# Cross attention with an expert layer: turning the first batch's token weights by VectorE and transfers instead of TensorE, and moving the third batch's token steps one group later

## The chip, the cores and the metric

The kernel runs on one core of a Trainium2 chip. The metric is the device time of one execution in microseconds (us). A program on one core has no second die to be compared with, so runs are told apart here by their time and by the mean granted TensorE clock that each run lists. Every repeated run counted as fast; the single runs of the three looks near the end have no state, and there the clock record itself decides.

Names in the profile: PE is TensorE's matmul stream, PEld its weight loads, DVE is VectorE, ACT is ScalarE, SP is SyncE; SPq and ACTq are the issuing of transfers by those two. L283 is line 283 of the kernel. The changed kernel's line numbers are mostly four higher than before: L415, L543, L593, L710, L716 before are L419, L547, L597, L714, L720 after. L197 (scores), L277 (read) and L283 (scaling of the read) are the same in both. The variants of the experiments have numbers of their own: L591 and L620 there are the L597 of the changed kernel, L541 is L547, L601 and L630 are L607, L278 is L277.

## The reference, cut to what matters

```python
# attention: B, H, S, Ns, D = 8, 8, 512, 32, 64, float32
scores  = scale * x @ state.T            # tokens look at states
a       = exp(scores - max); a /= sum + 1e-9
xread   = a @ state
scores2 = scale * state @ x.T            # states look at tokens
a2      = exp(scores2 - max); a2 /= sum + 1e-9
sread   = a2 @ x                         # "the read": needs a2 with tokens on partitions
# then, on concat(xread, sread) as 4608 rows of 512:
h = x @ w_in                             # 512 -> 2048
g = h * erf(softplus(h))
out = g @ w_out                          # 2048 -> 512
```

## The kernel before: the parts that matter here

Token weights `a2` come out of the softmax with states on partitions. The read needs them turned. The first batch turns them on TensorE, eight 128x128 transposes into two PSUM tiles (L261, 0.87 us on the chain); the other batches turn 32x32 blocks on VectorE (L370, 1.23 us) and let 16 transfers put the blocks in place (11.17 us of issuing for the second batch's).

```python
ps_at = ctx.enter_context(tc.tile_pool(name="ps_at", bufs=2, space=PSUM))   # two tiles "at"
...
    def turn_weights(a2):                        # first batch only
        a2T = att.tile([P, 2, NC, P], F32, name="sc")
        for e in range(2):
            ps = ps_at.tile([P, NC, P], F32, name="at")
            for c in range(NC):
                nc.tensor.transpose(out=ps[:, c, :], in_=a2[:, e, P * c:P * c + P],
                                    identity=ident)
            nc.scalar.copy(a2T[:, e], ps)
        return a2T
...
    def read_tokens(b, a2T, z2, pool=ps_at, name="at"):
        ...                                      # 64 small matmuls into one tile "at" (L277)
        for e in range(2):                       # L283 empties it
            nc.vector.tensor_scalar(sn[:, e], sr[:, e], z2[:, e:e + 1], None, op0=ALU.mult)
...
    def mixed_part(b, g, j, parts, ...):         # "mixing": takes both tiles "at"
        ps = [ps_at.tile([P, gw], F32, name="at")[:, 0:n] for _ in range(2)]
        ...
    def soft(i, gT):                             # ACT
        nc.scalar.activation(out=gT[0][:, i], in_=h_t[i], func=ACTF.Softplus)
    def keep_h(i, gT):                           # DVE, L710
        nc.vector.tensor_copy(gT[1][:, i], h_t[i])
    def evict(i, gT, late=False):
        for f in (keep_h, soft) if late else (soft, keep_h):
            f(i, gT)
```

Up to the point where the second batch's groups begin, the order of the source is the order on each engine. After it a scheduler orders the instructions, and steps of the next batch's attention are hung into the groups of matrix work as side steps (`side[k]`). From there on each group of matrix work forms the first layer from seven small products (L487) whose sums VectorE adds; "product two" and "product seven" below are two of them. The output matmuls (L593) of one group run between the products of the next.

Of the kernel before, what the change touches and what calls it, by code (L numbers as in the profile page):

```python
# [8 lines left out]
F32 = mybir.dt.float32  # L9
# [7 lines left out]
def kernel(  # L17
# [17 lines left out]
    nc = tc.nc  # L35
    B, H, S, D = x.shape
    Ns = state.shape[2]
# [187 lines left out]
    def sums(a):  # L225
        z1 = small.tile([P, 2, NC * NI], F32, name="z1")
        for e in range(2):
            nc.vector.reduce_sum(out=z1[:, e], in_=a[:, e], axis=AX.X)
        return z1
# [7 lines left out]
    def largest(sc):  # L237
        m2 = small.tile([P, 2], F32, name="m2")
        for e in range(2):
            nc.vector.reduce_max(out=m2[:, e:e + 1], in_=sc[:, e], axis=AX.X)  # L240
        nc.vector.tensor_scalar(m2, m2, -scale, None, op0=ALU.mult)
        return m2

    def weigh_tokens(sc, m2, a2):

        z2 = small.tile([P, 2], F32, name="z2")
        for e in range(2):
            nc.scalar.activation(out=a2[:, e], in_=sc[:, e], func=ACTF.Exp, bias=m2[:, e:e + 1],
                                 scale=scale, accum_out=z2[:, e:e + 1])
        return z2  # L250

    def inverse(z):
        nc.vector.tensor_scalar(z, z, 1e-9, None, op0=ALU.add)
        nc.vector.reciprocal(z, z)

    def turn_weights(a2):
        a2T = att.tile([P, 2, NC, P], F32, name="sc")
        for e in range(2):
            ps = ps_at.tile([P, NC, P], F32, name="at")
            for c in range(NC):  # L260
                nc.tensor.transpose(out=ps[:, c, :], in_=a2[:, e, P * c:P * c + P],  # L261
                                    identity=ident)
            nc.scalar.copy(a2T[:, e], ps)
        return a2T

    sn_t = {}
# [25 lines left out]
    def attention0(between):  # L292



        xt = x_t[0]
        xT = att.tile([P, NI, S], F32, name="xT")
        xp = [ps_o.tile([P, S], F32, name="o%d" % i) for i in range(3)]
        xp.append(ps_h.tile([P, S], F32, name="h"))
        for c in 1, 0, 2, 3:  # L300
            if c == 2:
                warm(3)
            for i in range(NI):
                nc.tensor.transpose(out=xp[i][:, P * c:P * c + P],
                                    in_=xt[:, c, 2 * i:2 * i + 2, :], identity=ident)
        for i in range(NI):
            (nc.scalar.copy, nc.vector.tensor_copy)[i % 2](xT[:, i, :], xp[i])
        states(range(1))
        s2 = scored(0, xT)
        between[0]()  # L310
        both = att.tile([P, NI, S], F32, name="xT")
        sc = att.tile([P, 2, S], F32, name="sc")
        a = states_weights(0, s2, both)
        for e in range(2):
            nc.scalar.copy(sc[:, e], s2[e])
        between[1]()
        z1 = sums(a)
        between[2]()
        normalise(a, z1)
        for e in range(2):  # L320
            nc.vector.transpose(out=aT[0][:, e], in_=both[:, e])

        def rest():
            a2 = both[:, 2:4]
            m2 = largest(sc)
            yield
            z2 = weigh_tokens(sc, m2, a2)
            inverse(z2)
            yield
            a2T = turn_weights(a2)  # L330
            yield
            read_tokens(0, a2T, z2)
            yield

        return rest()
# [9 lines left out]
    def attention(b, xT=None):  # L345



        turned = []
        if xT is None:  # L350
            xT, *turned = turn_x(b)
        sc, _ = scores(b, xT)
        marks.extend(turned)
        yield
        both = att.tile([P, NI, S], F32, name="xT")
        a = states_weights(b, [sc[:, e] for e in range(2)], both)
        yield
        m2 = largest(sc)
        yield
        z2 = weigh_tokens(sc, m2, both[:, 2:4])  # L360
        yield
        z1 = sums(a)
        inverse(z2)
        yield
        normalise(a, z1)
        for e in range(2):
            nc.vector.transpose(out=aT[b][:, e], in_=both[:, e])
        yield

        nc.vector.transpose(out=both[:, 0:2], in_=both[:, 2:4])  # L370
        a2T = att.tile([P, 2, NC, P], F32, name="sc")
        blocks = both[:, 0:2].rearrange("p e (c m n) -> p m (e c) n", m=NI, n=Ns)
        rows = a2T.rearrange("p e c (i n) -> p i (e c) n", n=Ns)
        for m in range(NI):
            for i in range(NI):
                nc.sync.dma_start(out=rows[Ns * m:Ns * m + Ns, i],
                                  in_=blocks[Ns * i:Ns * i + Ns, m])
        yield
        read_tokens(b, a2T, z2, *((ps_h, "h") if 1 < b < B - 1 else ()))
        if b + 1 < B:  # L380
            load_x(b + 1)
        yield
# [305 lines left out]
    def on_dve(kind, j, ks=range(3)):  # L688
        for k in ks:
            made[kind, j][1][k]()  # L690
            if k == 2:
                fetch()
# [51 lines left out]
    def some0(g, gT, rs, ts):  # L744
        done(project(gT[0], g, acc, rs, ts))
# [94 lines left out]
    def finish_(gT):  # L840
        for i in range(GF):
            erf(slice(i, i + 1), gT)
            times(slice(i, i + 1), gT)

    next(rest)
    finish_(g2)
    next(rest)
    on_dve("o", 5, [2])
    some0(2, g2, range(3), range(2))
    on_act("i", 6)  # L850
    next(rest)
# [2 lines left out]
    on_act("i", 7)  # L854
    m_t[0, 3] = mix.tile([P, 2, gw], F32, name="m")
    mixed_part(0, 3, 0, 2, nc.scalar.copy, nc.scalar.copy)
    xT, _ = turn_x(1)
    some0(2, g2, range(1), range(2, 4))
    on_dve("i", 7, [0, 1])
    next(rest)  # L860
    on_dve("i", 7, [2])
    load_x(1)
    on_act("o", 6)
    on_dve("o", 6, [0, 1])
    turn = attention(1, xT)
# [11 lines left out]
    next(turn)  # L877
    on_dve("o", 6, [2])
    next(turn)
    some0(2, g2, range(1, 2), range(2, 4))  # L880
    for i in 2, 3:
        first0(3, i, g3[0])
        evict(i, g3)
    some0(2, g2, range(2, 3), range(2, 4))
    finish_(g3)
    mixed(1, 2 * begins(1), nc.scalar.copy, nc.scalar.copy)
    some0(2, g2, range(3, 4), range(2, 4))
# [31 lines left out]
    for b in range(1, B + 1):  # L919
        if b < B:  # L920
            groups = fast(b, 2, lambda h, b=b: put_x(b, h))
        else:
            groups = fast(b, 1, lambda h: put_s)
        for g, (first, second) in enumerate(groups):
            side = {}
            if b in (1, B - 1) and g == 0:
                side[2] = lambda turn=turn: next(turn)
            if 1 < b < B and g == 0:
                side[3] = lambda: behind(marks, combine_m, b, 1 - begins(b))
            if b + 1 < B:  # L930

                late = b == 1
                if g == late:
                    side[6 if late else 6] = (lambda: behind(marks, next, turn)) if late else \
                        lambda old=turn: (next(old), behind(marks, next, turn))
                    turn = attention(b + 1)
                if g == 1 + late:
                    side[1] = lambda: next(turn)
                    side[7] = lambda: behind(marks, lambda: [next(turn) for _ in range(5)])
                if g > 1:  # L940
                    o = g - 2 ^ begins(b + 1)
                    side[5] = lambda: mixed_pair(b + 1, (2 * o, 2 * o + 1))
                    if g == 3:
                        side[6] = lambda: behind(marks, combine_a, b + 1)
                        side[3] = lambda: behind(marks, combine_m, b + 1, begins(b + 1))
            elif b + 1 == B and g == 1:
                side[4] = lambda: [turn_read(range(k, min(k + 4, B))) for k in range(0, B, 4)]
            elif b + 1 == B and g > 1:

                if g == 2:  # L950
                    side[6] = lambda: combine_a(B)
                side[8] = lambda: combine_s(g - 2 ^ begins(B))
            steps = accompanied(pending(), side)
            copy = [nc.vector.tensor_copy] if (b, g) == (1, 1) else []
            gT_ = first(lambda: next(steps), *copy)
            if b == 1 and g == 0:
                combine_m(1, 1 - begins(1))
                behind(marks, combine_w, begins(1), 1, 2)
            if b == 1 and g == 1:
                behind(marks, combine_w, begins(1), 4, 3)  # L960
            done(steps)
            if b == 1 and g == 1:
                behind(marks, combine_w, 1 - begins(1), 1, 2, 4, 3)

            def pending(gT=gT_, second=second):
                return second(gT)
# [31 lines left out]
```

## Time and profile before

| | before |
|---|---|
| time, median of the first 3 runs | 734.76 us (734.64 to 735.06) |
| PE busy | 98% of the span |
| holes in PE's stream from 80 to 176 us, by steps from start to start | 3.5 us in all |

PE's busy share leaves nothing to win but PE work and holes, and the holes are too short for the page's slices. So they are read from PE's timeline: a row gives start, length, line, operation, shapes, how many instructions follow one another, and in brackets how long PE was idle before it and what ended that. The lines are in the prediction below.

### The profile page before, as it was taken

What the parts mean: (1) busy time and instruction counts of PE and PEld (TensorE: products, weight loads), DVE (VectorE), ACT (ScalarE), POOL (GpSimd) and SP (SyncE); (2) the same over time, 40 slices, a digit from 0 to 9 for tenths busy, and PEclk for the clock granted to TensorE, in tenths of its full rate; (3) what the DMA queues carried; (4) which work ended last, traced back from release to release, by engine and by line L of the source; (5) the groups of instructions that cost most, each with busy time, mean ns of one, the idle gap of its engine ahead of it and who ended that gap; (6) DMA issues with size and microseconds to landing.
All of it is one profiled execution on the core that took longest, in us unless ns stands there. A gap on an engine that the chain in (4) does not pass through costs nothing.

```text
span 733.0 us, 12127 instructions
## 1 busy us (share of the span) xinstructions
PE 721.4 (98%) x5016; PEld 587.0 (80%) x5016; DVE 523.7 (71%) x765; ACT 397.0 (54%) x499; POOL 0.7 (0%) x6
## 2 busy tenths in 40 slices
PE   8899999999999999999999999999999999999998
PEld 7434435878889888988989888988898899999996
DVE  4987887998698666867587669866686756675423
ACT  4898894657455445754355445554565434443340
POOL 0000000000000000000000000000000000000000
PEclk9999999999999999999999999999999999999999
DMA  7587842331152201410061104220121000000001
GB/s 233 175 244 213 218 95 58 87 58 21 38 97 55 53 1 44 102 30 30 1 144 23 37 1 93 57 43 13 26 62 30 30 1 30 1 30 1 30 1 29
DMA packets 139166, 46.40 MB, mean 63 GB/s; under 512 B 126696, under 2 KB 130536, under 8 KB 139112
## 3 DMA queue, kind: packets, MB, share of 16 engines
q1 hardware_dynamic: 136840, 44.92, 24.7%
q10 hardware_dynamic: 2272, 0.72, 0.5%
q8 instruction: 39, 0.64, 0.4%
q14 instruction: 15, 0.12, 0.1%
HBM read 33.03 MB, written 8.91 MB: 57 GB/s over the span
## 4 chain that ended last, share of the span: by engine, by line
PE 87%; DVE 6%; ACT 2%; issue 1%; DMA 0%; SPq 0%; DVEq 0%; ACTq 0%
PE o L593 48%; PE h L487 26%; PE o L543 6%; PE at L401 2%; PE h L401 1%; PE h L703 1%; PE at L197 1%; PE at L415 1%; PE h L277 1%; DVE hs L495 1%; DVE raw L569 1%; DVE s L538 1%; DVE s L716 0%; DVE hs L710 0%; DMA out_dram<-ot 0%
## 5 line engine op out<-in xcount | busy, mean ns | idle before, releaser
L593 PE MATMUL o<-w_out,s 128*128 128x256 f32 x480 | 118.2, 380 | 0.9 <-DVE ot L603 0.5
L593 PE MATMUL o<-raw,hs 128*128 128x256 f32 x480 | 117.0, 382 | 0.0
L494 ACT ACTIVATE s<-hs 128x512 f32<-128x512 f32 x120 | 75.3, 630 | 76.1 <-DVE hs L495 75.7
L593 PE MATMUL o<-w_out,hs 128*128 128x256 f32 x480 | 114.0, 380 | 0.2 <-DVE hs L592 0.2
L593 PEld LDWEIGHTS o<-raw,hs 128*128 128x128 f32 x480 | 90.0, 190 | 22.5 <-issue 10.9
L495 DVE TENSOR_TENSOR hs<-hs,h 128x512 f32<-128x512 f32 x90 | 61.7, 686 | 63.7 <-PE h L487 63.7
L593 PEld LDWEIGHTS o<-w_out,hs 128*128 128x128 f32 x480 | 90.6, 190 | 16.8 <-issue 4.2
L593 PEld LDWEIGHTS o<-w_out,s 128*128 128x128 f32 x480 | 84.6, 191 | 9.2 <-DVE ot L603 0.7
L495 DVE TENSOR_TENSOR hs<-s,h 128x512 f32<-128x512 f32 x60 | 41.0, 683 | 68.9 <-PE h L487 68.4
L487 PEld LDWEIGHTS h<-aT,m 128*128 128x128 f32 x672 | 83.9, 192 | 4.7 <-issue 1.4
L487 PE MATMUL h<-aT,m 128*128 128x128 f32 x672 | 84.7, 275 | 0.2 <-ACT s L498 0.2
L538 DVE TENSOR_TENSOR s<-s,hs 128x2048 f32<-128x2048 f32 x30 | 68.5, 2284 | 19.9 <-ACT s L537 19.9
L498 ACT COPY s<-h 128x512 f32<-128x512 f32 x29 | 17.0, 585 | 113.3 <-PE h L487 113.3
L543 PE MATMUL o<-w_out,s 128*128 128x512 f32 x128 | 59.0, 600 | 0.6 <-DVE s L716 0.5
L487 PE MATMUL h<-sy,sx 128*128 128x128 f32 x448 | 59.1, 275 | 0.0
L503 ACT COPY hs<-h 128x512 f32<-128x512 f32 x29 | 17.0, 585 | 76.1 <-PE h L487 76.1
L487 PEld LDWEIGHTS h<-sy,sx 128*128 128x128 f32 x448 | 56.6, 192 | 1.8 <-issue 0.5
L537 ACT ACTIVATE s<-s 128x2048 f32<-128x2048 f32 x30 | 57.4, 1912 | 0.3
L593 PE MATMUL o<-raw,s 128*128 128x256 f32 x240 | 56.8, 379 | 0.0
L543 PEld LDWEIGHTS o<-w_out,s 128*128 128x128 f32 x128 | 23.1, 190 | 30.7 <-issue 25.8
L593 PEld LDWEIGHTS o<-raw,s 128*128 128x128 f32 x240 | 43.5, 190 | 4.8
L494 ACT ACT_TABLE_LOAD x31 | 39.8, 1283 | 0.5
(130 smaller groups left out, 912.0 us busy)
## 6 DMA issues: line engine op xcount, KB each, us to landing
raw<-in_moe_w_in_dram SPq DMA_DIRECT2D x8, 1024.0 KB, 5.6
raw<-in_moe_w_out_dram SPq DMA_DIRECT2D x8, 1024.0 KB, 4.9
xq<-in_x_dram SPq DMA_DIRECT2D x112, 64.0 KB, 2.2
x<-in_x_dram SPq DMA_DIRECT2D x56, 128.0 KB, 2.8
out_dram<-ot SPq DMA_DIRECT2D x18, 256.0 KB, 2.2
sc<-xT SPq DMA_DIRECT2D x112, 32.0 KB, 1.9
out_dram<-ot SPq DMA_DIRECT2D x28, 128.0 KB, 1.8
x<-in_x_dram SPq DMA_DIRECT2D x2, 256.0 KB, 5.0
```

The costliest lines, as they stand in the source:

```text
L197: on_pe = nc.tensor.matmul(out=s2[e][q, :], lhsT=st[r, b, q], rhs=xT[r, i, :], start=True, stop=True)
L277: nc.tensor.matmul(out=sr[q, e, :], lhsT=a2T[:, e, c, q], rhs=xt[:, c, 2 * i + e, :], start=(c == 0), stop=(c == NC - 1))
L401: nc.tensor.matmul(out=ps[k][e][q, :], lhsT=st[r, b, q], rhs=w_in[r, 2 * g:2 * g + 2, i, :], start=True, stop=True)
L487: last = nc.tensor.matmul(out=bank[:, q], lhsT=lhsT, rhs=rhs, start=(first and i == 0 and k == 0), stop=(i == GF - 1 and k == len(ops) - 1 ...
L494: nc.scalar.activation(out=s[:, k], in_=hs[:, k], func=ACTF.Softplus)
L495: add = lambda o, x, y: nc.vector.tensor_tensor(o, x, y, op=ALU.add)
L498: copy(m1, p)
L503: copy(c11, p)
L537: return (nc.scalar.activation(out=s, in_=s, func=ACTF.Erf), nc.vector.tensor_tensor(s, s, hs, op=ALU.mult))
L538: nc.vector.tensor_tensor(s, s, hs, op=ALU.mult))
L543: nc.tensor.matmul(out=acc[r], lhsT=gT[:, i, P * r:P * r + P], rhs=w_out[:, GF * g + i, :], start=(g == 0 and i == 0), stop=(g == NG - 1 a ...
L593: nc.tensor.matmul(out=acc[bank][:, E2 * c:E2 * c + E2], lhsT=lhs[:, i, :], rhs=rhs[:, g, i, :], start=(first and i == 0 and c == 0), stop ...
```

## The change

Its intent is to take 0.87 us of transposes off TensorE and to make TensorE's holes smaller. Part one: the first batch's weights go the way of the other batches, the second batch's scores come before the first batch's read, and the read comes behind the last first-layer products, to leave time for 16 transfers. Part two: the third batch's token steps (largest, exponential, sum, turn, transfers) move one group later. The core of the diff:

```diff
-    def turn_weights(a2):
-        ... (eight TensorE transposes, two ScalarE copies)
+    def move_weights(both, a2T):
+        blocks = both[:, 0:2].rearrange("p e (c m n) -> p m (e c) n", m=NI, n=Ns)
+        rows = a2T.rearrange("p e c (i n) -> p i (e c) n", n=Ns)
+        for m in range(NI):
+            for i in range(NI):
+                nc.sync.dma_start(out=rows[Ns * m:Ns * m + Ns, i],
+                                  in_=blocks[Ns * i:Ns * i + Ns, m])
@@ first batch
-            a2T = turn_weights(a2)
+            turned = mix.tile([P, 3, gw], F32, name="sx", bufs=2)[:, 0:2]
+            nc.vector.transpose(out=turned, in_=a2)
+            yield
+            a2T = ...
+            move_weights(turned, a2T)
@@ the read of the first batch
-    next(rest)
-    on_dve("i", 7, [2])
-    load_x(1)
...
     for i in 2, 3:
         first0(3, i, g3[0])
         evict(i, g3)
-    some0(2, g2, range(2, 3), range(2, 4))
+    next(rest)
+    load_x(1)
     finish_(g3)
     mixed(1, 2 * begins(1), nc.scalar.copy, nc.scalar.copy)
@@ third batch
+        if b == 2:
+            z2 = weigh_tokens(sc, largest(sc), both[:, 2:4])     # now behind the state weights
+            inverse(z2)
...
-                    side[7] = lambda: behind(marks, lambda: [next(turn) for _ in range(5)])
+                    side[7] = lambda: behind(
+                        marks, lambda: [next(turn) for _ in range(1 if late else 5)])
+                if late and g == 3:
+                    side[7] = lambda: behind(marks, next, turn)
```

More of the change, by code (lines that the diff above doesn't have):

```diff
@@ L254, in inverse @@
         nc.vector.reciprocal(z, z)
-    def turn_weights(a2):
-        a2T = att.tile([P, 2, NC, P], F32, name="sc")
-        for e in range(2):
-            ps = ps_at.tile([P, NC, P], F32, name="at")
-            for c in range(NC):
-                nc.tensor.transpose(out=ps[:, c, :], in_=a2[:, e, P * c:P * c + P],
-                                    identity=ident)
-            nc.scalar.copy(a2T[:, e], ps)
+    def move_weights(both, a2T):
[5 more added lines that the diff above has]
+                                  in_=blocks[Ns * i:Ns * i + Ns, m])
         return a2T
@@ L329, in rest @@
             yield
-            a2T = turn_weights(a2)
+            turned = mix.tile([P, 3, gw], F32, name="sx", bufs=2)[:, 0:2]
+            nc.vector.transpose(out=turned, in_=a2)
+            yield
+            a2T = mix.tile([P, 3, gw], F32, name="sx", bufs=2)[:, 0:2].rearrange(
+                "p e (c t) -> p e c t", t=P)
+            move_weights(turned, a2T)
             yield
@@ L357, in attention @@
         yield
-        m2 = largest(sc)
-        yield
-        z2 = weigh_tokens(sc, m2, both[:, 2:4])
-        yield
-        z1 = sums(a)
-        inverse(z2)
-        yield
+        if b == 2:
+            z1 = sums(a)
+        else:
+            m2 = largest(sc)
+            yield
+            z2 = weigh_tokens(sc, m2, both[:, 2:4])
+            yield
+            z1 = sums(a)
+            inverse(z2)
+            yield
         normalise(a, z1)
@@ L368, in attention @@
         yield
+        if b == 2:
+            z2 = weigh_tokens(sc, largest(sc), both[:, 2:4])
+            inverse(z2)
         nc.vector.transpose(out=both[:, 0:2], in_=both[:, 2:4])
-        a2T = att.tile([P, 2, NC, P], F32, name="sc")
-        blocks = both[:, 0:2].rearrange("p e (c m n) -> p m (e c) n", m=NI, n=Ns)
-        rows = a2T.rearrange("p e c (i n) -> p i (e c) n", n=Ns)
-        for m in range(NI):
-            for i in range(NI):
-                nc.sync.dma_start(out=rows[Ns * m:Ns * m + Ns, i],
-                                  in_=blocks[Ns * i:Ns * i + Ns, m])
+        a2T = move_weights(both, att.tile([P, 2, NC, P], F32, name="sc"))
         yield
@@ L846 @@
     finish_(g2)
+    on_dve("o", 5, [2])
     next(rest)
-    on_dve("o", 5, [2])
     some0(2, g2, range(3), range(2))
@@ L856 @@
     mixed_part(0, 3, 0, 2, nc.scalar.copy, nc.scalar.copy)
+    next(rest)
     xT, _ = turn_x(1)
     some0(2, g2, range(1), range(2, 4))
-    on_dve("i", 7, [0, 1])
-    next(rest)
-    on_dve("i", 7, [2])
-    load_x(1)
+    on_dve("i", 7)
     on_act("o", 6)
@@ L879 @@
     next(turn)
-    some0(2, g2, range(1, 2), range(2, 4))
+    some0(2, g2, range(1, 3), range(2, 4))
     for i in 2, 3:
@@ L883 @@
         evict(i, g3)
-    some0(2, g2, range(2, 3), range(2, 4))
+    next(rest)
+    load_x(1)
     finish_(g3)
```

## The prediction

> **What bounds the kernel now.** I read the page's busy shares and slices first, then the chain of waits, then the PE, DVE and SP timelines from 76 to 220 us, the only stretch in which the diff moves anything.
>
> ```profile
> PE 721.4 (98%) x5016; PEld 587.0 (80%) x5016; DVE 523.7 (71%) x765; ACT 397.0 (54%) x499; POOL 0.7 (0%) x6
> ...
> PE   8899999999999999999999999999999999999998
> ...
> PE 87%; DVE 6%; ACT 2%; issue 1%; DMA 0%; SPq 0%; DVEq 0%; ACTq 0%
> ```
>
> PE is full from the second slice to the last, so only two things can be won: PE work removed, and holes in PE's stream. The chain leaves PE in 13% of the span, and after 176 us it hardly leaves it. The part for the first and second batch, from the chain of waits for 82 to 110 us (start, length, what):
>
> ```profile
> 82.93 0.87 PE at L261 x8
> 83.81 1.72 PE o L543 x4
> 85.52 0.59 PE at L415 x16
> 86.12 1.91 PE o L543 x4
> 88.03 1.03 PE at L277 x64
> 89.06 1.86 PE at L197 x16
> ...
> 92.69 1.30 DVE xT L217 x2
> ...
> 104.92 0.70 DVE s L716
> ...
> 105.67 1.98 PE o L543 x4
> ```
>
> L261 is the turning that the change removes, L277 the first batch's read, L197 the second batch's scores. The same 16 score matmuls take 1.02 us at 208 us, so the 1.86 here holds 0.8 us of waiting: L197 needs the PSUM tile that the read filled and DVE empties (L283). From 90.9 to 105.6 the chain runs through DVE and ACT: whatever delays the second batch's softmax there delays the next output matmuls. The later holes, from PE's timeline:
>
> ```profile
> 135.77 2.86 PE L593 MATMUL o<-w_out,s 128*128 128x256 f32 x12 [0.35 <-DVE s L538]
> ...
> 161.63 1.99 PE L593 MATMUL o<-w_out,hs 128*128 128x256 f32 x8 [0.21 <-DVE hs L592]
> ...
> 174.20 0.71 PE L487 MATMUL h<-aT,m 128*128 128x128 f32 x4 [0.24 <-ACT s L498]
> 175.43 1.99 PE L593 MATMUL o<-w_out,s 128*128 128x256 f32 x8 [0.53 <-DVE ot L603]
> ```
>
> Bracketed idle understates them, as ends are modelled. By steps from start to start (a 128x512 matmul every 0.429 us, 256 columns every 0.216, 128 every 0.112) the holes are about 0.8 at L197, 0.3 at 96.4, 0.4 at 104.8, 0.5 at 135, 0.4 at 161, and 1.1 us at 173.7 to 175.4: 3.5 us in all.
>
> DVE's timeline holds the two rows on which my argument rests, and SP's the price of a shuffle:
>
> ```profile
> 84.98 2.30 DVE L339 STREAM_TRANSPOSE xT<-xq 128x2048 f32<-128x2048 f32 x1
> ...
> 102.49 1.29 DVE L710 COPY hs<-h 128x512 f32<-128x512 f32 x2 [0.96 <-ACT s L707]
> ```
> ```profile
> 112.23 11.17 SPq L376 DMA_DIRECT2D sc<-xT  x16
> ```
>
> [...]the other batches have just this pair (L370 for 1.23 us, then the 16 transfers). [...]L710 waits 0.96 us for ACT's softplus L707[...]. [...]the page shows 1283 ns for 31 loads. [...]the first batch's exponential starts at 78.81, 1.30 us after its load did at 77.51. [...]DMA is 0.76 busy there and SP issues one each 0.7 us, so SP's order matters more.
>
> **Part one, first batch.** Removed: 8 transposes, 0.87 us of PE on the chain, and two ACT copies (1.07 us). Added: one DVE turn of 128x1024 (1.15 us, half of 2.30), 16 transfers (about 11 us of SP), no PE work. The order of instructions shows that DVE does a weight step (L149, 1.13 us) while it formerly idled 1.89 us before L253 at 80.36, so the DVE chain does not grow.
>
> PE reaches the mixing L415 at 84.5, but its weights are ready only at 85.06 (L149, 83.83 + 1.23), so 0.6 of the 0.87 us turns into a wait. Then output matmuls to 87.6; scores, now before the read, end at 88.6 instead of 90.8. DVE is still busy with weights until 92.15, so L217 starts only 0.5 us earlier than its 92.69; DVE and ACT run 0.3 to 0.5 us ahead. PE finishes everything up to the last first-layer matmuls by 100.0 and reads by 101.0. The shuffle can be issued from 85.5 (behind the second w_out load) to about 96.5 and lands 1.9 us later, at 98.4: in time.
>
> But the read's tile is emptied by DVE only after both copies L710, and those wait for softplus. ACT's softplus comes after the exponentials (98.5 to 100.1) and a table load (to 101.4): first one to 102.0, copies to 103.25, read scaled by 103.7. The next mixing matmuls need that tile. So PE waits 101.0 to 103.75: 2.7 us. After it: mixing 1.02, four output matmuls 1.8, and the output group that started at 105.67 starts at 106.6. Net of part one: +0.9 us, despite the removed PE work.
>
> **The stretch to 154 us.** All this shifts by 0.9. The read of the second batch, formerly at 132.33, between two products that wait for DVE, moves about 11 us later in PE's order. Its 1.03 us had filled a hole: now product seven waits for its addend until 133.8 (0.8 us), and the output matmuls wait for L538 (shifted to 136.5) from 135.65 to 136.6 (0.95, was 0.5). The group is then again 0.9 late, with the 1.03 us of reading still owed: +1.9. ACT's two output copies come after an Erf ending at 145.3, against PE's arrival at 145.7: perhaps 0.2 more.
>
> **Part two, third batch.** Nothing is removed. Its max (1.2 us of DVE), two exponentials and a table load or two of ACT, the inversion, the 1.23 us turn and 16 transfers leave the group of 150 to 175 and go to the next, where DVE was idle 2.2, 2.8 and 1.1 us from 193 to 203. ACT loses the exponentials with their tables before and after Erf, so Erf runs about 165.7 to 167.6 instead of 168.4 to 170.3. DVE then multiplies by 170, and the store's first sum is done by 174.7, against PE at 175.6. The holes at 161 and 173.7 to 175.4 (1.5 us) nearly vanish; a wait of 0.3 remains at 160. In exchange the shuffle starts at about 196.6, ends at 196.6 + 10.4 + 1.9 = 208.9 at the latest, and the read, moved about 2.6 us back, comes at 209.9: hidden, with 1 us to spare.
>
> **Sum.** By this replay PE starts at 175.6 the output group that began at 175.43, and has 0.45 us of product still to do that the old order had done: +0.6 us. After that nothing changes. So 735.4 by the sum. I shade it to 734.9: an error in the order of ACT and DVE work around 101 us can only be worth up to its 2.7 us, and mostly in the favourable direction.
>
> **Rivals.** First, PE's work decides: no new wait, 0.87 saved and most holes closed. At most 0.87 + 3.5 = 4.4 us, 730.4 us. For it: PE is 98% busy and part two makes slack just where DVE held PE. Against it: the order puts the mixing directly behind the read, and L710's wait is in the trace. A middle case, the release at 101 comes early but the later hole stays, gives about 732.7. Second, transfers: if the first shuffle lands late, PE waits at the read, but up to about 2 us of that are covered by the wait that I expect anyway; a delay of 4 us would make 737. The trace speaks against it, as 16 xq transfers took 9.72 us in this place. Third, the third batch's shuffle comes later than 210 us: a delay of 1 us costs 1 us, about 736. Fourth, DVE becomes the bound in the group from 176 to 200 us: its idle of 6 us there against about 3 us of added work speaks against it.
>
> **Range and chances.** 734.9 us, 8 in 10 between 733.0 and 736.4. Two per cent are 14.7 us, over three times what all holes and the removed work together are worth, and a loss of that size needs a transfer to stall PE ten times longer than a shuffle's landing. Faster by over 2%: 0.005; within 2%: 0.985; slower: 0.01.
>
> **What would show it.** The eight L261 transposes and two L263 copies gone. The scores before the read, ending near 88.6. PE idle 2 to 3 us before the mixing that follows the first read, ended by DVE's scaling of it. Holes near 133 and 136 larger than before, those at 161 and 174 gone. The third shuffle landed before its read. No change in PE's rhythm after 215 us. I am wrong if PE goes on straight after the first read (the time is then near 732.5), or if a read waits for a transfer.

## The result, and the profile after

The changed kernel takes 736.47 us, median of 6 runs (736.02 to 737.88); before, on the same chip, 734.82 us (734.64 to 735.06, 6 runs). The ratio is 1.0027, with a 95% interval of 1.0015 to 1.004. Ratios are the mean time of one kernel's fast runs over that of the other's of the same rounds, so not quite the ratio of the medians quoted. The change costs about 1.7 us: same within 2%, but 0.07 us above the range that was predicted.

The six runs fall in two bunches: four from 736.02 to 736.57 us at a mean clock of 0.999 or 1.0, and two at 737.87 and 737.88 us, both at 0.998. Such runs are called long, the others undisturbed, below. The profiled run is the lowest of the six.

The page's busy row of the changed kernel:

```profile
PE 720.5 (98%) x5008; PEld 585.9 (80%) x5008; DVE 525.6 (72%) x766; ACT 392.6 (53%) x494; POOL 0.7 (0%) x6
```

PE lost its eight transposes (5016 to 5008 instructions, 0.9 us of busy time), yet the execution got longer: the gain was more than spent on waits. PE's timeline of the changed kernel shows the first of them:

```profile
84.96 0.67 PE L419 MATMUL at<-w_in,st 64*32 64x256 f32 x16 [0.55 <-DVE w_in L149]
...
87.47 1.09 PE L197 MATMUL at<-xT,st 64*32 64x512 f32 x16
...
101.12 1.04 PE L419 MATMUL at<-w_in,st 64*32 64x512 f32 x2
```
```profile
103.71 1.09 PE L419 MATMUL at<-w_in,st 64*32 64x512 f32 x14 [1.54 <-DVE sn L283]
```

Most of the removed transposes' time comes back at once as a wait of 0.55 us for the weights of the mixing. Then the read ends near 101.1; the mixing puts out 2 of its 16 matmuls, those into the free tile, and stands until 103.71, when VectorE has scaled the read and so emptied the other tile. The idle time in brackets counts a modelled end; by steps from start to start 2.1 us are lost. The chain of waits says why it took VectorE until then:

```profile
98.43 1.52 ACT xT L248 x4
...
99.96 1.28 ACT L711
...
101.26 0.61 ACT s L711
...
101.89 1.29 DVE hs L714 x2
103.18 0.40 DVE sn L283 x2
```

Read from the bottom: the scaling L283 stands behind two copies L714 on VectorE's queue, these wait for ScalarE's softplus (L711), and that for a table load (1.28 us from 99.96, with the softplus starting at 101.26) and the second batch's exponentials (L248). Nothing in this chain is what the scaling itself needs; it only stands behind it. Later, where the second batch's read was formerly in PE's order:

```profile
133.75 1.16 PE L491 MATMUL h<-aT,m 128*128 128x128 f32 x8 [0.57 <-DVE hs L499]
...
136.55 1.99 PE L597 MATMUL o<-w_out,s 128*128 128x256 f32 x8 [0.75 <-DVE s L542]
...
175.43 1.89 PE L597 MATMUL o<-w_out,s 128*128 128x256 f32 x8
```

Holes at 133 and 136 that were smaller or absent, and none any more at 173 to 175: part two did what it was meant to do there. The third batch's read, before and after, from PE's timelines of the two kernels:

```profile
206.97 1.10 PE L277 MATMUL h<-x,sc 128*32 128x64 f32 x64
208.00 1.09 PE L197 MATMUL at<-xT,st 64*32 64x512 f32 x16
```
```profile
209.91 1.23 PE L277 MATMUL h<-x,sc 128*32 128x64 f32 x64
...
212.04 1.03 PE L597 MATMUL o<-w_out,hs 128*128 128x256 f32 x4
213.15 1.09 PE L197 MATMUL at<-xT,st 64*32 64x512 f32 x16
```

Before, the scores follow the read 1.03 us after its start. After the change four output matmuls from 211.07 on and four more stand between them, the read takes 1.16 us from its start to the next matmul, and the scores start at 213.15. Four output matmuls from 212.04 at 0.216 us end at 212.9, and going over to matmuls of another shape takes about 0.1 us more, as before the read at 206.97, so 213.0 was possible. What they waited for is on VectorE, here after the change:

```profile
210.79 2.31 DVE L344 STREAM_TRANSPOSE xT<-xq 128x2048 f32<-128x2048 f32 x1
```

The turn of the next batch's tokens, 2.3 us, started at 204.83 before: it stands 6 us later. And SP's row for the third shuffle:

```profile
196.47 11.60 SPq L262 DMA_DIRECT2D sc<-xT  x16
```

SP spends 11.60 us on these 16 issues of 32 KB, 0.73 us each on average. The last of them begins at 207.5 us (`--source L262`), and with the 1.9 us from issue to landing that the page gives for these transfers it lands at about 209.4, half a microsecond before the read. The stretches around it (`--windows 208.5:209,209.5:210`) confirm that. A line has a stretch, its length, the engines' busy times with numbers of instructions, the clock, and in the last two columns the busy share of the DMA engines and GB/s:

```profile
208.50:209.00 0.50, 0.50 (x4) 0.43 (x3) 0.42 (x1) 0.04 (x1) 0.00 (x0) 1.00 0.40 65
209.50:210.00 0.50, 0.50 (x8) 0.17 (x7) 0.50 (x1) 0.02 (x1) 0.00 (x0) 1.00 0.00 0
```

So the read did not wait for the shuffle. In two more profiles of the changed kernel, taken later, the read takes its former 1.03 us and the scores alone wait, for the turn; why it took 1.16 here is not known. The kernel's text shows why the turn comes late: the pool `att` has one buffer for the tile `xT`, the shuffle's transfers read from it and the next turn writes it, so the turn cannot start before the shuffle is through. It then stands directly behind the multiplication L542 on VectorE's queue; before the change, and in the experiment below with the third batch's steps earlier, it stands ahead of it. That is read from the kernel and the order of instructions, not tested with a second buffer.

Compared instruction by instruction, PE in the profiled run runs 0.24 us ahead of the kernel before at 72 us, ahead of everything that moved, 0.34 us behind at 177 us, 0.83 us behind at 217 us and 0.92 us behind at the end: the change costs 0.58 us up to 177 us and another 0.58 us after that, 0.5 of them between 207 and 217 us. About 0.2 of these 0.5 us are no wait: the read and the scores no longer follow each other, so PE changes over to another shape twice more, at 0.1 us each (in the trace of before such a step takes 0.31 or 0.32 instead of 0.22 us).

### The profile page after: what moved, and what is told of

Read it like the earlier page. It is cut to its first block, busy times and chain, and to the rows that moved or that the text cites. A ratio compares the mean times of both kernels' runs of the same rounds, so it can differ in the third digit from the quotient of the medians.

```text
span 734.2 us, 12121 instructions
## 1 busy us (share of the span) xinstructions
PE 720.5 (98%) x5008; PEld 585.9 (80%) x5008; DVE 525.6 (72%) x766; ACT 392.6 (53%) x494; POOL 0.7 (0%) x6
## 4 chain that ended last, share of the span: by engine, by line
PE 83%; DVE 2%; ACT 1%; issue 1%; DVEq 0%; ACTq 0%
PE o L597 49%; PE h L491 27%; PE o L547 2%; PE at L405 2%; PE h L405 1%; PE at L197 1%; PE at L419 1%; PE h L277 1%; DVE s L542 0%; DVE hs L714 0%; DVE xT L344 0%; DVE hs L499 0%; PE at L277 0%; ACT s L541 0%; ACT xT L248 0%
## 5 line engine op out<-in xcount | busy, mean ns | idle before, releaser
L542 DVE TENSOR_TENSOR s<-s,hs 128x2048 f32<-128x2048 f32 x30 | 68.6, 2285 | 19.9 <-ACT s L541 19.9
L502 ACT COPY s<-h 128x512 f32<-128x512 f32 x29 | 17.0, 586 | 103.6 <-PE h L491 102.0
```

Of the source, the lines that this page charges most:

```text
L502: copy(m1, p)
L542: nc.vector.tensor_tensor(s, s, hs, op=ALU.mult))
```

## The experiments

The theories. A: an idle microsecond of PE costs a microsecond; the sum of the holes (101, 133 and 136, 207 to 217) is the whole loss. D: besides, in some runs TensorE's granted clock is halved for a while behind the hole at 101 us (as the traces of the longer hole and of a disturbed run below show, at 0.50), which makes the second bunch of runs. The rivals: part one costs nothing but part two does, through the late shuffle; or the long runs are ordinary scatter, or lose their time elsewhere.

### Part one alone

The changed kernel with the third batch's steps back where they were:

```diff
-        if b == 2:
-            z1 = sums(a)
-        else:
-            m2 = largest(sc); ...
+        m2 = largest(sc); ...
-                        marks, lambda: [next(turn) for _ in range(1 if late else 5)])
-                if late and g == 3:
-                    side[7] = lambda: behind(marks, next, turn)
+                    side[7] = lambda: behind(marks, lambda: [next(turn) for _ in range(5)])
```

> Only the first batch's part of the change; the third batch's steps stay where they were. Theory A (PE waits for the PSUM tile of the first read, and the second batch's read no longer fills a hole): the same 2.5 us PE hole before the mixing at 101 us as in the changed kernel, the hole at 135 us still there, and the holes of before at 161 and 173.7 to 175.4 us back (1.5 us), while the read and the scores near 210 us wait for nothing (0.5 to 0.9 us saved): about 737.0 us, between 736.3 and 737.8, so at least as slow as the whole change. Rival B (the later shuffle of the third batch is what costs): near 734 us.

Measured: 738.97 us median of 5 (737.51 to 739.51), against 734.84 us of before; ratio 1.0051 (1.0039 to 1.0064). Two runs at full clock took 737.51 and 737.71 us, near the expectation's upper end; three at a clock of 0.996 or 0.997 took 738.97 to 739.51 us, which theory A doesn't have. The loss is part one's, and part two takes back about 1.2 us of it (737.6 to 736.4 at full clock). How, PE's timeline says: without part two the late group waits longer than before at 175 us.

```profile
177.33 0.92 PE L591 MATMUL o<-w_out,s 128*128 128x256 f32 x3 [1.53 <-DVE ot L601]
```

### Part two alone

The kernel before with part two's lines of the diff only.

> Only the third batch's part; the first batch as before. Theory A: the holes at 161 and 173.7 to 175.4 us go (1.5 us), 0.5 to 0.9 us come back near 210 us at the third read and the scores behind it: about 733.9 us, between 733.3 and 734.5, faster than the kernel before by about 1 us. Rival B: 736 us or more, with PE holes near 210 us of 2 us.

Measured: 734.23 us (734.08 to 734.31, 5 runs), ratio 0.9991 (0.9977 to 1.0005). The median is 0.6 us below before, and all five runs are below all nine of before (734.75 to 735.03), though the interval includes 1. The rival by which part two carries the loss falls.

### The scaling ahead of the copies

```diff
     for i in 2, 3:
         first0(3, i, g3[0])
-        evict(i, g3)
+        soft(i, g3)
     next(rest)
+    for i in 2, 3:
+        keep_h(i, g3)
```

The read and VectorE's scaling now stand ahead of the two copies; what each of them needs is unchanged, only the place in the queue is another.

> The whole change, but VectorE scales the first read ahead of the two copies that wait for softplus; same instructions, same work, TensorE's order untouched. Theory A: the hole before the mixing shrinks from 2.5 us to about 0.6 us; some of it moves to the wait for the products at 105 us; the time falls by 1.0 to 1.6 us to about 735.1 us. Rival C (the 16 transfers of the first shuffle and what queues behind them set the time): no change, 736.4 us.

Measured: 735.10 us (735.02 to 735.19, 5 runs), as expected, and no long run. The two rows of PE's timeline that held the wait have become one:

```profile
101.38 1.84 PE L419 MATMUL at<-w_in,st 64*32 64x512 f32 x16
```

16 matmuls in a row instead of 2 and 14. Between the second and the third of them 0.3 us are left of the 2.1. So 1.8 us came from the place of the scaling in VectorE's queue. The gain is smaller than that, 1.3 us against undisturbed runs: the output matmuls at 105 us wait for the multiplications L720 in any case, as they did before the change.

### The second batch's read pinned to its old place

PE and VectorE keep, in the second batch's second group, the order that they had before: the read between products two and seven.

```diff
-        between()
-        product(2, p, False)
+        on_pe = product(2, p, False)
         copy(c11, p)
-        product(7, q, False)
+        with ExitStack() as held:
+            held.enter_context(tc.issue_after(reads[1]))    # the read's last matmul
+            on_pe = product(7, q, False)
         ... (the following products, additions and output matmuls likewise held behind)
```

> The whole change, but the second batch's read is held in its old place of TensorE's order, between the two products that wait for VectorE, and VectorE's order there is the old one. Theory A: the hole of 0.7 us at 133 us is filled by the read, the one at 135.5 us stays at 0.5 to 0.9 us, so 0.7 to 1.0 us are saved: about 735.6 us. Rival C: the read comes too early for its transfers, TensorE waits at it, and nothing is saved: 736.4 us or more.

Measured: 735.60 us median (735.39 to 737.27, 5 runs), ratio 1.0018. Three runs at full clock, 735.39 to 735.60; two at 0.998, 737.12 and 737.27. The read is back in the hole:

```profile
133.24 1.10 PE L278 MATMUL at<-x,sc 128*32 128x64 f32 x64
...
136.68 2.64 PE L620 MATMUL o<-w_out,s 128*128 128x256 f32 x11 [0.36 <-DVE s L559]
```

No wait at 133 any more, and 0.36 in place of 0.75 us before the output matmuls: about 1.0 us gained at full clock. The hole at 101 us was left, and so were the long runs. So far a kernel with that hole had long runs, and a kernel without it had none.

### The hole made longer

The opposite of the third experiment: the read and its scaling go behind the four multiplications of the group.

```diff
+    finish_(g3)
     next(rest)
     load_x(1)
-    finish_(g3)
```

> Dose of the hole. The changed kernel with the read of the first batch and its scaling put behind the four multiplications of the fourth first-layer product, so VectorE empties the read's PSUM tile at about 107 us instead of 103.7. Theory A (the tile of the read decides, an idle TensorE microsecond costs one microsecond and nothing else): PE is held from about 101.6 to 107.3, some 3.5 us more than in the changed kernel, so about 739.8 us, the same in all runs. Theory D[...]: the granted clock falls visibly near 104 to 112 us in the trace[...], so 740.4 to 741.6 us, in most runs and not in two of five as now. Rival (the hole is filled by other ready work of PE): no change, 736.5 us.

Measured: 742.86 us (742.63 to 743.28, 4 runs; a fifth is not on record), all at a clock of 0.995; ratio 1.011 (1.0094 to 1.0125). All runs are long and none is at full clock. Stretches of this run, each with its length, then the busy time of PE, PEld, DVE, ACT and POOL with numbers of instructions, then the granted clock (PEclk), the DMA share and GB/s:

```profile
105.60:109.00 3.40, 1.24 (x14) 0.25 (x14) 3.33 (x9) 0.66 (x2) 0.00 (x0) 0.50 0.75 134
109.00:112.40 3.40, 3.40 (x11) 1.20 (x5) 3.35 (x5) 2.62 (x4) 0.00 (x0) 0.50 1.04 234
112.40:116.00 3.60, 3.60 (x23) 1.24 (x22) 2.67 (x3) 0.73 (x2) 0.00 (x0) 1.00 0.44 78
```
```profile
107.76 1.96 PE L419 MATMUL at<-w_in,st 64*32 64x512 f32 x14 [5.18 <-DVE z L232]
```

The last of these lines is from PE's timeline: PE stands until 107.76. The clock is 0.50 from 105.6 to 112.4, for 6.8 us, and 1.00 in the stretches before and after. In the column of instructions 11 go by in the last half-clock stretch and 23 in the next. PE was not idle throughout: it was busy for 0.58 us from 102.0 to 105.6 and for 1.24 us from 105.6 to 109.0. The bill, an estimate from these lengths: the hole is 3.64 us longer (5.76 instead of 2.12), and of the time at half clock, which lasts to 112.43 in the clock record, PE worked 112.43 - 107.76 = 4.67 us; at a clock of 0.50 half of that is lost, 2.3 us. Together 6.0 us over the 736.5 of undisturbed runs make 742.5; 0.4 us of the median remain unaccounted for, and 0.1 us of the profiled run (742.63). Theory D named the drop of the clock, but its range ended at 741.6 us. Theory A alone, 739.8 us, is 3 us short.

### Both mends together

The third and fourth experiments in one kernel.

> The two mends of before together on the whole change: scaling of the read ahead of the two copies, and the second batch's read pinned between products two and seven. If the two holes are separate terms, their gains against the changed kernel add (736.4 to 735.1 by the first, to 735.6 by the second): 733.7 to 734.2 us, no run more than 0.3 us above the others. Rival (with the first hole gone the group after it starts earlier and the next wait takes the gain back): about 735.0 us.

Measured: 734.49 us (734.16 to 734.54, 5 runs), ratio 0.9993 (0.998 to 1.0005); no long run. The sum of the two gains (1.3 and 1.0 us against undisturbed runs) promised 734.1; 0.3 us were given back. The expected range is missed by that much at its upper end, and the rival's 735.0 by more. The kernel is 2 us better than the changed one, but it does not clearly beat the kernel before (all five runs are below its nine, 734.77 us and more, but the interval includes 1), nor part two alone.

### The third batch's steps earlier in their group

```diff
-                    side[7] = lambda: behind(marks, next, turn)
+                    side[1] = lambda: behind(marks, next, turn)
```

on top of both mends: the shuffle of the third batch starts sooner.

> As the kernel with both mends, and the third batch's token steps come at the second place of their group instead of the eighth, so that its 16 transfers start about 4 us or more sooner. If the lag found near 210 to 215 us is the read and the scores waiting for late transfers and a late turn, 0.4 to 0.5 us come off: 733.2 to 733.8 us. Rival (VectorE's work at the group's start delays the additions that the output matmuls wait for): 734.0 to 735.0 us, with a new hole between 176 and 190 us.

Measured: 734.95 us (734.90 to 735.17, 5 runs), 0.5 us worse than both mends alone. The scores' wait went, as the theory said, but its forecast was wrong. PE with the steps late, then with the steps sooner:

```profile
173.43 1.99 PE L620 MATMUL o<-w_out,s 128*128 128x256 f32 x8
...
211.24 1.09 PE L197 MATMUL at<-xT,st 64*32 64x512 f32 x16 [0.21 <-DVE xT L347]
```
```profile
175.12 1.99 PE L620 MATMUL o<-w_out,s 128*128 128x256 f32 x8 [0.47 <-DVE ot L630]
...
207.69 1.09 PE L197 MATMUL at<-xT,st 64*32 64x512 f32 x16
```

The wait before the scores is gone; they follow the read directly, as in the kernel before. But a hole as before the change is back at 175.1, for the store's sum on VectorE. In numbers: aligned instruction by instruction, the second kernel lags the first by 0.1 us at 172 us, by 1.25 us at 184 us and by 0.67 us at the end. So the hurry near 207 to 217 us is worth 0.58 us, the size of the loss found there in the changed kernel, and it costs 1.1 us at 175 us. The traces tell the turn and the transfers apart: with the steps late the read takes 1.04 us, as ever, and its transfers landed 1.1 us before it, so only the scores waited, for the turn (L347). With the steps sooner the turn starts at 204.52 us instead of 208.88.

### The changed kernel once more, and looks at single runs

The changed kernel unaltered:

> The changed kernel once more on this chip, for the spread of its runs. Theory D: runs fall in two bunches, 736.0 to 736.6 us at a mean clock of 0.999 to 1.0 and 737.5 to 738 at 0.998, about one in three in the second; a trace that falls in the second shows TensorE's granted clock below 1.0 in a window just behind the hole at 101 us. Rival (ordinary scatter): no such bunches, or the clock is the same in both.

Measured: 736.71 us (736.46 to 738.37, 5 runs): three at full clock from 736.46 to 736.71, two at 0.997 and 0.998 with 738.26 and 738.37. The two bunches are there, but the profiled run was an undisturbed one, so where a disturbed run loses its time was still not seen. Hence three single looks.

> A look to catch a disturbed run of part one alone, three of five of which had a mean clock of 0.996 to 0.997 and took 1.3 to 2.0 us longer. Theory D: in a disturbed run the clock record shows TensorE at half speed[...], and the steps of PE in that stretch are doubled; nowhere else does the run lose time. An undisturbed run is 737.5 us with one unbroken record. Rival: a disturbed run loses its time elsewhere (a late transfer, a longer start), and the drop of the clock is not at the hole.

> As the look at part one alone, with the changed kernel: 736.0 to 736.7 us in an unbroken clock, or 737.9 to 738.4 us (about one run in three) with half the clock[...] beginning between 101 and 107 us. Rival: a run of 738 us with an unbroken clock, or with the drop elsewhere.

> Once more part one alone, as before: 737.5 us with an unbroken clock or 738.9 to 739.5 us with half the clock near 102 to 110 us. Rival: a long run with an unbroken clock, or the drop elsewhere.

Measured: 739.24 us at a clock of 0.997 (part one), 736.35 at 1.0 (the changed kernel), 737.64 at 1.0 (part one). The first is a disturbed run with its trace, the third its undisturbed twin: the same kernel in the same batch of runs on one chip. Stretches of the disturbed run, then of its twin:

```profile
104.00:106.00 2.00, 2.00 (x15) 0.67 (x16) 1.39 (x3) 2.00 (x4) 0.00 (x0) 0.66 0.73 122
106.00:108.00 2.00, 2.00 (x3) 0.67 (x2) 1.93 (x5) 2.00 (x4) 0.00 (x0) 0.50 0.72 122
```
```profile
106.00:108.00 2.00, 2.00 (x6) 0.95 (x5) 1.93 (x5) 2.00 (x4) 0.00 (x0) 1.00 0.74 122
```

From 106 to 108 us PE is "busy" in both, but 3 matmuls go by in one and 6 in the other: busy share says nothing of the clock. The eight output matmuls behind the mixing, disturbed and undisturbed:

```profile
105.32 5.04 PE L541 MATMUL o<-w_out,s 128*128 128x512 f32 x8
```
```profile
105.07 3.70 PE L541 MATMUL o<-w_out,s 128*128 128x512 f32 x8
```

They begin 0.25 us later and take 1.34 us longer: 1.6 us, the whole difference of the two runs (739.24 - 737.64). After that the two traces run in step to the end. The clock records, in us from the span's start:

```
disturbed   full 5.66 to 104.64, half 104.64 to 108.06, full 108.06 to 736.11
undisturbed full 6.70 to 737.15
```

The half clock lasts 3.42 us and begins within 0.7 us after the hole's end at 103.99. This is theory D, seen. The rivals fall, at least for this run.

How often does it come? The kernels with this hole of 2.1 us (the changed one, part one, the pinned read) had 24 runs, 10 of them long at a lower clock (0.996 to 0.998). The kernels without it (before in the two timed batches, whose longest hole from 80 to 110 us is 0.8 us, part two, early scaling, both mends with and without sooner steps) had 38 runs, none long. One thing is open: in the first profiled run of part one PE was busy for 0.96 us from 101.5 to 104.0 us, exactly as in the disturbed run, and its clock stayed at 1.00. So the hole alone isn't enough; what decides between two such runs was not shown.

## Why the prediction was right or wrong

The steps that failed are two terms of the sum that were set at 0: that "in exchange" for part two's gain the third shuffle is "hidden, with 1 us to spare", and that "after that nothing changes". The first measured 0.58 us: the shuffle itself was in time, but the scores waited for a turn that the step did not look at, and no longer followed the read. The second measured 0.33 us at the kernel's end, by a cause that stays open. With them the sum's 735.4 becomes 736.3 us, the mean of the four undisturbed runs. The prediction had also taken 0.5 us off its sum for an unmeasured reason, and had no term for the half clock. The median lies above the range only because two of six runs were long: the four others have a median of 736.34 us, just inside. By its own steps:

- "The scores before the read, ending near 88.6": measured 87.47 to 88.49. The transposes and their copies are gone. Of the 0.87 us that they took, 0.6 turned into a wait as stated (0.55 in brackets). Right.
- "PE waits 101.0 to 103.75: 2.7 us": PE's next matmul starts at 103.71, released by the scaling, with the chain that was predicted link by link: exponentials, table load, softplus, copies, scaling. By steps 2.1 us are lost, as two of the mixing's matmuls got through first. Right; early scaling shows that this place in the queue is the cause.
- "Product seven waits ... 0.8 us" and 0.95 us before the output matmuls: by steps from start to start 0.73 and 0.91 us. Right; the pinned read shows the cause.
- "The holes at 161 and 173.7 to 175.4 nearly vanish": they did. "+0.6 us" at 175: measured 0.58 us, counted from PE's position at 72 us in both traces. Right.
- "The read ... comes at 209.9: hidden, with 1 us to spare": for the transfers that was right. The read comes at 209.91 and they landed about 0.5 us before it, 1.1 us in the look at the changed kernel (209.2 against 210.24). But the move isn't free: the turn of the next batch's tokens, which needs the shuffle's buffer and on which the scores wait, was not in the step at all, nor that the scores would no longer follow the read directly. The term was set at 0 and measured 0.58 us; with the steps sooner the same amount comes back. (The step also counted the 1.9 us from the end of the issuing; the trace counts them from the start of each issue.)
- "After that nothing changes": PE's rhythm does not, but the end does. From PE's last matmul to the end of the span it was 3.59 us before and 3.91, 4.24 and 3.91 us in the three profiles of the changed kernel. Columns of the rows below: what is transferred, from which queue, number, KB each, median us from issue to landing; before and then the changed kernel's second profile.

```profile
out_dram<-ot SPq DMA_DIRECT2D x2, 64.0 KB, 1.9
```
```profile
out_dram<-ot SPq DMA_DIRECT2D x2, 64.0 KB, 2.5
```

The last stores were issued later behind PE's end and landed more slowly. Every profile of a kernel with part one has 3.88 us or more, part two alone 3.60; the cause stays open.

- "I shade it to 734.9: ... mostly in the favourable direction": the sum said 735.4. Correcting downwards by 0.5 us for an unknown error had no measurement behind it, and every term found missing went the other way. That the third rival named "about 736" is luck: its delay of the shuffle did not come.
- A small slip: 14.7 us are not ten but about eight times a shuffle's landing (14.7 / 1.9). Nothing rests on it.

With the profile from the single look at the changed kernel the sum closes: 0.08 us that PE was late already at 72 us, 0.59 up to 177, 0.58 from there to its last matmul, 0.33 in the tail: 1.58 us. Its span is 734.57 us, before 732.99. On top of that, in 4 of 12 runs of the changed kernel, come about 1.7 us at a lower mean clock, 0.997 or 0.998 (the mean of those four is 738.1 us, of the eight others 736.4); the half clock itself was traced only in part one and with the longer hole. No step of the prediction had this term: it priced a hole at its length. It lifts the median of the six first runs by 0.13 us only, as four of them were undisturbed, but it lifts the mean of twelve by about 0.55 us.

## What to carry to other kernels

A PSUM tile's emptying should be placed in an engine's queue by when its data is ready, not where the source happens to have it: here one scaling of 0.40 us behind two copies that wait for another engine held PE for some 1.8 us, and moving two lines won 1.3 us of the time. Removing work from the busiest engine is worth little where its next operand is late (here 0.6 of 0.87 us came back as a wait), so first ask what it will wait for next. And two things cost more than they seem to: behind a hole of some 2 us the granted clock can fall (0.50 for 3.42 us in the traced run of part one; 10 of 24 runs with that hole were long), and work that is moved later takes along whatever needs its buffer, here the turn of the next batch's tokens, so a step that is "hidden with 1 us to spare" is a term to be priced, not a zero.
